# Rewriting a tuned attention and gated-MLP kernel as one scheduled graph: query projections behind the kv sum, paired 64-row remainders, first chunk in halves

## Chip, cores, metric

One core of one Trainium2 chip. The metric is device time in microseconds (us), lower is better. "Span" is the time from the first to the last instruction of one profiled execution; a timed execution is about 1.7 us longer than its own span (238.04 against 236.3). "Granted clock" is the share of TensorE's full clock that the profile recorded. In the lines of the profile PE stands for TensorE's matmuls, PEld for its weight loads, DVE for VectorE, ACT for ScalarE, POOL for GpSimd; a bracket at the end of a line gives the idle time before it and what ended it. PSUM is the memory that matmuls write to; the kernel uses it as eight banks of 512 columns. A run's *state* is fast or slow by its time and clock.

## The reference

A pre-norm block on 2048 tokens of width 448: linear attention with 16 heads of 28 and a softmax feature map, then a gated MLP of width 1792. All inputs are bf16. Abridged:

```python
def _A_ref(x, wqkv, w_phi, wo):
    # q, k, v of x @ wqkv, 16 heads of 28
    pq = jnp.einsum("bhsd,hdf->bhsf", q, w_phi)
    pk = jnp.einsum("bhsd,hdf->bhsf", k, w_phi)
    phi_q = concat([softmax(pq), softmax(-pq)])
    phi_k = concat([softmax(pk), softmax(-pk)])
    kv = jnp.einsum("bhsf,bhsd->bhfd", phi_k, v)   # sum over all tokens: "the kv sum"
    z  = jnp.einsum("bhsf->bhf", phi_k)
    num = jnp.einsum("bhqf,bhfd->bhqd", phi_q, kv)
    den = jnp.einsum("bhqf,bhf->bhq", phi_q, z)[..., None] + 1e-6
    return (num / den).reshape(B, S, D) @ wo

h  = x + _A_ref(layernorm(x), wqkv, w_phi, wo)
h2 = h + (sigmoid(layernorm(h) @ w_gate) * (layernorm(h) @ w_up)) @ w_down
```

Both kernels work in 16 *tiles* of 128 tokens and in *chunks* of four tiles. "num" is the matmul of query features with the kv sum, "item" one block of 128 of the 1792 MLP columns (14 items a chunk) for gate and up together, "down" the last projection, which accumulates 14 matmuls a tile. The width of 448 is three blocks of 128 rows and a remainder of 64: gate and up each need three 128-row matmuls and one 64-row matmul per item. The 64-row matmuls of gate and of up use different halves of the array and can run side by side (in the trace of the kernel before both start at 199.71). The projection matrices of q and k are first multiplied by w_phi in the kernel ("preparation" of the q and k weights).

## The kernel before

The first part is written out by step (a tile per step), with half of the query projections, those of chunks 0 and 1, placed among the steps ahead of the kv sum:

```python
NPQ_A = min(NCH, 2)
for c in range(NPQ_A):
    for g in range(G):
        pq_at.setdefault(4 * c + 3 + O_XT + 1 + 2 * g, []).append((g, c))
pq_deferred = [(g, c) for c in range(NPQ_A, NCH) for g in range(G)]
```

Behind the kv sum, ACT copies num out of PSUM before VectorE works on it:

```python
def a3_copy(t):
    # [cut: waits]
    tk = mark(s_act, act.copy(opm_sb[:, t % NSO, :, :, :].rearrange("p b h e -> p b (h e)"), opm_psum(t)), ("om", t))
```

One gate and up item: two times three full matmuls, then the two 64-row matmuls. ACT takes the sigmoid and copies u, GpSimd multiplies:

```python
def b_gu(f, c):
    # [cut: waits]
    for kt in range(3):
        pe.matmul(banks[bg][:, 0:512], lhsT=wg_sb[:, kt, f * P:(f + 1) * P], rhs=hnT[:, kt, cs], start=(kt == 0), stop=False)
    for kt in range(3):
        pe.matmul(banks[bu][:, 0:512], lhsT=wu_sb[:, kt, f * P:(f + 1) * P], rhs=hnT[:, kt, cs], start=(kt == 0), stop=False)
    pg = pe.matmul(banks[bg][:, 0:512], lhsT=wg_sb[0:64, 3, f * P:(f + 1) * P], rhs=hnT[0:64, 3, cs], start=False, stop=True)
    pu = pe.matmul(banks[bu][:, 0:512], lhsT=wu_sb[64:P, 3, f * P:(f + 1) * P], rhs=hnT[64:P, 4, cs], start=False, stop=True, tile_position=(64, 0))

def b_ucp(f, c):
    tk = mark(s_act, act.copy(u_sb[:, j % 2, :], banks[bu][:, 0:512]), ("ucp", (f, c)))

def b_hh(f, c):
    tk = mark(s_pool, pool.tensor_tensor(hhTc[c][:, f, :], sg_sb[:, j % 2, :], u_sb[:, j % 2, :], ALU.mult), ("hh", (f, c)))
```

The softmax here doesn't subtract the row's maximum and nothing guards it: scores larger than these inputs give would overflow.

## Time and profile before

| | before |
|---|---|
| time, median of 3 runs | 254.34 us (253.8 to 255.51) |
| span of the profiled run, mean granted clock of TensorE | 252.2 us, 0.972 |
| busy: TensorE, VectorE, ACT, GpSimd | 223.5, 127.6, 131.4, 129.9 us |
| exp of tile 0 starts | 15.36 us |
| kv sum masked, ready for num | 63.8 us |
| first gate matmul | 93.44 us |
| last matmul ends, and what follows it | 248.25 us, 4.0 us |

The share of busy time hides that the kernel has three stages with different limits; the last three rows are the borders of these stages.

### The profile page before, as it was taken

What the parts mean: (1) busy time and instruction counts of PE and PEld (TensorE: products, weight loads), DVE (VectorE), ACT (ScalarE), POOL (GpSimd) and SP (SyncE); (2) the same over time, 40 slices, a digit from 0 to 9 for tenths busy, and PEclk for the clock granted to TensorE, in tenths of its full rate; (3) what the DMA queues carried; (4) which work ended last, traced back from release to release, by engine and by line L of the source; (5) the groups of instructions that cost most, each with busy time, mean ns of one, the idle gap of its engine ahead of it and who ended that gap; (6) DMA issues with size and microseconds to landing.
All of it is one profiled execution on the core that took longest, in us unless ns stands there. A gap on an engine that the chain in (4) does not pass through costs nothing.

```text
span 252.2 us, 3761 instructions
## 1 busy us (share of the span) xinstructions
PE 223.5 (89%) x1248; PEld 106.2 (42%) x1248; DVE 127.6 (51%) x344; ACT 131.4 (52%) x258; POOL 129.9 (51%) x145
## 2 busy tenths in 40 slices
PE   1889999994769769979889999899999999999992
PEld 1555656553446334423233454234533345434340
DVE  3566999984497999999999631000100002000003
ACT  2547778871276979945655601763055550154350
POOL 8215687876122445868888601675037660154531
PEclk9999999998668999999999999999999999999999
DMA  6799567530022352332232321000100001100002
GB/s 162 202 326 310 137 171 137 128 83 3 0 42 43 64 106 47 70 73 48 48 67 52 75 62 36 3 0 1 54 19 3 0 3 36 36 1 3 0 0 73
DMA packets 37899, 17.18 MB, mean 68 GB/s; under 512 B 29304, under 2 KB 36984, under 8 KB 37880
## 3 DMA queue, kind: packets, MB, share of 16 engines
q1 hardware_dynamic: 37880, 16.94, 27.6%
q8 instruction: 10, 0.16, 0.3%
q14 instruction: 9, 0.07, 0.1%
HBM read 8.28 MB, written 1.84 MB: 40 GB/s over the span
## 4 chain that ended last, share of the span: by engine, by line
PE 53%; DVE 30%; issue 5%; DMA 5%; ACT 3%; POOL 2%; POOLq 0%; DVEq 0%; ACTq 0%; SPq 0%
PE bank L41 53%; DVE ssum L41 5%; DVE hn_pad L41 5%; DVE mv L41 4%; DVE h_sb L41 3%; DVE rr L41 3%; DVE rden L41 2%; DVE b_sb L41 2%; DMA xnT_50<-xn_pad 2%; DVE xn_pad L41 2%; DVE st L41 2%; POOL phi L41 2%; DMA wqkv_sb<-in_A_wqkv_dram 2%; DVE c_sb L41 1%; DMA x_51<-in_A_x_dram 1%
## 5 line engine op out<-in xcount | busy, mean ns | idle before, releaser
L41 PE MATMUL bank<-hnT,wg_sb 128*128 128x512 bf16 x224 | 65.5, 382 | 4.3 <-ACT u_sb L41 3.5
L41 ACT ACTIVATE sg_sb<-bank 128x512 bf16<-128x512 f32 x56 | 33.4, 596 | 66.8 <-PE bank L41 62.4
L41 PE MATMUL bank<-hnT,wu_sb 128*128 128x512 bf16 x224 | 63.4, 381 | 0.0
L41 DVE TENSOR_TENSOR h_sb<-bank,h_sb 128x448 bf16<-128x448 f32 x16 | 9.7, 623 | 94.6 <-PE bank L41 94.6
L41 PEld LDWEIGHTS bank<-hnT,wg_sb 128*128 128x128 bf16 x224 | 18.6, 96 | 46.9 <-issue 30.7
L41 POOL TENSOR_TENSOR mv<-mv,neghalf 128x1 f32<-128x1 f32 x32 | 18.8, 589 | 33.4 <-DVE mv L41 33.3
L41 ACT CAST u_sb<-bank 128x512 bf16<-128x512 f32 x56 | 32.4, 581 | 0.0
L41 POOL TENSOR_TENSOR hhT_64<-sg_sb,u_sb 128x512 bf16<-128x512 bf16 x14 | 16.2, 1154 | 26.9 <-ACT u_sb L41 26.9
L41 PEld LDWEIGHTS bank<-hnT,wu_sb 128*128 128x128 bf16 x224 | 21.6, 96 | 19.8
L41 POOL TENSOR_TENSOR phi<-ek,ssum 128x896 bf16<-128x896 bf16 x16 | 27.1, 1703 | 1.6 <-DVE ssum L41 1.6
L41 POOL TENSOR_TENSOR hhT_60<-sg_sb,u_sb 128x512 bf16<-128x512 bf16 x14 | 16.1, 1153 | 18.6 <-ACT u_sb L41 18.6
L41 POOL TENSOR_TENSOR o_pad<-c_sb,rden 128x448 bf16<-128x448 bf16 x16 | 15.0, 940 | 18.9 <-DVE rden L41 17.1
L41 POOL TENSOR_TENSOR hhT_56<-sg_sb,u_sb 128x512 bf16<-128x512 bf16 x14 | 16.1, 1159 | 15.4 <-ACT u_sb L41 15.1
L41 ACT CAST opm_sb<-bank 128x960 bf16<-128x960 f32 x16 | 15.6, 975 | 14.1 <-PE bank L41 13.9
L41 DVE TENSOR_SCALAR hn_pad<-h_sb,mv 128x448 bf16<-128x448 bf16 (+1 forms) x32 | 19.7, 659 | 1.3 <-POOL mv L41 1.3
L41 DVE TENSOR_REDUCE ssum<-ek 128x32 f32<-128x896 bf16 x16 | 17.1, 1070 | 2.7 <-ACT ek L41 2.7
L41 POOL TENSOR_TENSOR hhT_52<-sg_sb,u_sb 128x512 bf16<-128x512 bf16 x14 | 17.0, 1217 | 1.6 <-ACT u_sb L41 1.6
L41 PE MATMUL bank<-wo_sb,oT 112*128 112x448 bf16 x64 | 15.6, 367 | 1.9 <-DMA oT<-o_pad 1.0
L41 ACT ACTIVATE junk<-h_sb 128x448 bf16<-128x448 bf16 x16 | 9.4, 588 | 14.4 <-DVE h_sb L41 14.4
L41 ACT ACTIVATE ek<-bank 128x448 bf16<-128x448 f32 x32 | 16.0, 568 | 0.0
L41 DVE TENSOR_TENSOR b_sb<-opm_sb,rr 128x464 bf16<-128x464 bf16 x16 | 13.8, 864 | 0.6
L41 PE MATMUL bank<-wd_sb,hhT_64 128*128 128x448 bf16 x56 | 12.8, 355 | 0.8 <-POOL hhT_64 L41 0.8
(101 smaller groups left out, 309.3 us busy)
## 6 DMA issues: line engine op xcount, KB each, us to landing
out_dram<-h_sb SPq DMA_DIRECT2D x16, 112.0 KB, 1.7
wd_sb<-in_B_w_down_dram SPq DMA_DIRECT2D x7, 224.0 KB, 3.3
wg_sb<-in_B_w_gate_dram SPq DMA_DIRECT2D x3, 448.0 KB, 5.9
wu_sb<-in_B_w_up_dram SPq DMA_DIRECT2D x3, 448.0 KB, 3.9
wqkv_sb<-in_A_wqkv_dram SPq DMA_DIRECT2D x3, 392.0 KB, 3.7
x_51<-in_A_x_dram SPq DMA_DIRECT2D x2, 224.0 KB, 3.0
x_55<-in_A_x_dram SPq DMA_DIRECT2D x1, 448.0 KB
x_59<-in_A_x_dram SPq DMA_DIRECT2D x1, 448.0 KB
```

Source lines behind the costliest of these rows:

```text
L41: ins = getattr(eng, op)(*args, **kw)
```

## The change

The intent: build the whole kernel as one graph of operations with durations and priorities, order it with a list scheduler, and use the freedom for six things. (1) An early start: one tile of x first, filler matmuls. (2) The normalization of the first layer norm moves from VectorE to ACT, its small vectors are done for up to four tiles at once. (3) All 16 query projections go behind the kv sum. (4) VectorE reads num from PSUM and also takes the product of gate and up, so that two kinds of ACT copies and GpSimd's product go. (5) Two items form a pair whose four 64-row matmuls can stand next to each other. (6) The first chunk is cut in halves, so two finished tiles are enough for the first gate matmul. The diff has 1705 lines; its core:

```diff
@@ query projections: 8 of 16 ahead of the kv sum -> all behind it, by priority @@
-            pq_deferred = [(g, c) for c in range(NPQ_A, NCH) for g in range(G)]
+        NPRE = 4
+        pql = [(c, gg) for c in range(NCH) for gg in range(G)]
+        for i, (c, gg) in enumerate(pql[:NPRE]):
+            pq(c, gg, 4 + i % 2, 10 - i * 0.1)
[... cut ...]
+        for i, (c, gg) in enumerate(pql[NPRE:]):
+            pq(c, gg, (4, 5)[i % 2], 12 - i * 0.1)
@@ small vectors of the first layer norm by groups @@
+        groups = [[0], [1], [2, 3]] + [list(range(4 * c, 4 * c + 4)) for c in range(1, NCH)]
@@ chunks @@
+        chunks = [(0, 2), (2, 2)] + [(4 * c, 4) for c in range(1, NCH)]
@@ one item; j is its place in the pair @@
+            def pair(e, st):
+                e.matmul(bk(bg)[:, 0:N], lhsT=wg_sb[0:64, 3, fs], rhs=hb[0:64, 3, ns], start=st, stop=not st)
+                return e.matmul(bk(bu)[:, 0:N], lhsT=wu_sb[64:P, 3, fs], rhs=hb[64:P, 3, ns], start=st, stop=not st,
+                                tile_position=(64, 0))
+            if j == 0:
+                def fn(e):
+                    full(e, wg_sb, bg, True, False)
+                    full(e, wu_sb, bu, True, False)
+                    return pair(e, False)
[... cut: the op "gu" ...]
+            else:
+                def fn1(e):
+                    pair(e, True)
+                    return full(e, wg_sb, bg, False, True)
+
+                def fn2(e):
+                    return full(e, wu_sb, bu, False, True)
[... cut: the ops "gg" and "uu" ...]
@@ product: GpSimd from two SBUF tiles -> VectorE from PSUM @@
-                tk = mark(s_act, act.copy(u_sb[:, j % 2, :], banks[bu][:, 0:512]), ("ucp", (f, c)))
[... cut ...]
-                tk = mark(s_pool, pool.tensor_tensor(hhTc[c][:, f, :], sg_sb[:, j % 2, :], u_sb[:, j % 2, :], ALU.mult),
[... cut ...]
+            op("dve", "hh%d_%d" % (ci, ff), lambda e: e.tensor_tensor(
+                hhT[(t0 // 4) % NHH][:, ff, ns], bk(bu)[:, 0:N], sg_sb[:, k, 0:N], ALU.mult),
@@ down: three chunks in one bank @@
+                if last:
+                    down(t, (3, 2, 6, 7)[i], [2] * 7, 10 - i)
+                else:
+                    down(t, 3, [4, 4, 3, 3], 10)
```

The first item of a pair (op "gu") ends with its 64-row matmuls, the second ("gg", then "uu") begins with them.

## The prediction

> **What bounds the kernel now.** I first cut the span into stretches in the view of engine busy time by window, at the places where the chain of waits changes its engine (us from the start, length, busy time of PE, PEld, DVE, ACT, POOL, granted clock, DMA share, GB/s):
>
> ```profile
> 25.00:55.00 30.00, 29.43 (x219) 18.02 (x217) 27.78 (x65) 23.67 (x52) 23.13 (x20) 1.00 0.60 138
> 55.00:64.00 9.00, 4.44 (x44) 3.16 (x42) 5.15 (x14) 2.65 (x6) 6.10 (x4) 0.82 0.01 2
> 64.00:93.40 29.40, 22.41 (x152) 13.60 (x150) 23.28 (x79) 21.64 (x38) 8.83 (x11) 0.82 0.25 50
> 93.40:130.00 36.60, 34.15 (x183) 13.45 (x184) 35.00 (x100) 23.20 (x47) 26.74 (x29) 1.00 0.30 61
> 160.00:248.30 88.30, 87.26 (x424) 35.51 (x424) 5.58 (x10) 35.94 (x68) 40.32 (x35) 1.00 0.03 11
> ```
>
> There are three regimes. Up to 64 us the first layer norm, the k and v projections and the kv sum. From 64 to 93.4 the attention output without any gate or up matmul to fill TensorE: the first one is at 93.44 in the timeline. From 93.4 to 248.3 the rest, with TensorE nearly always fed. So the end is set by two things: when the first gate matmul can start, and how densely TensorE works from there.
>
> Then the chain of waits in order of time (start, length, what), one period of the first regime:
>
> ```profile
> 26.86 0.50 DVE st L41
> 27.38 0.19 DVE mv L41
> 27.67 0.16 DVE mv L41
> 27.86 0.40 DVE xn_pad L41
> 28.25 1.01 DVE ssum L41
> 29.29 0.35 DVE ssum L41
> 29.64 0.50 DVE st L41
> ```
>
> Statistics, three small vectors, the normalization (0.40), the softmax sums (1.01) and their reciprocal (0.35): 2.78 us a tile, all on VectorE. The "PE busy 29.43" beside it is overlapped matmuls, not a full array.
>
> Last the timeline of TensorE late in the kernel (start, length, engine, operation), one gate and up item:
>
> ```profile
> 198.31 0.82 PE L41 MATMUL bank<-hnT,wg_sb 128*128 128x512 bf16 x3
> 198.97 0.81 PE L41 MATMUL bank<-hnT,wu_sb 128*128 128x512 bf16 x3
> 199.71 0.39 PE L41 MATMUL bank<-hnT,wg_sb 64*128 64x512 bf16 x1
> 199.71 0.39 PE L41 MATMUL bank<-hnT,wu_sb 64*128 64x512 bf16 x1
> 200.03 0.82 PE L41 MATMUL bank<-hnT,wg_sb 128*128 128x512 bf16 x3
> ```
>
> Item to item 1.72. The six full matmuls pace at 0.218 (0.66 for three). The two 64-row matmuls start together, so they are already concurrent. But they start 0.74 after the up triple instead of 0.655, and the next item starts 0.32 later instead of 0.218: 0.19 us an item goes into entering and leaving the 64-row mode.
>
> **What the skill says.** (1) TensorEngine Tiling (Array Packing), Key Properties: "Changing tiling mode (not just tile) drains the TensorE". The 0.19 above agrees. (2) TensorE: Matmul & The Clock Gate, Part 1: an array with too little to do is gated to half rate and comes back after a few busy microseconds. The trace agrees: 448-column matmuls pace 0.37 until about 23 us and 0.19 later, and the granted clock is 0.82 over the two stretches from 55 to 93.4. (3) VectorE: DVE Perf Modes, Why PSUM operands drop a tier: fp32 from PSUM runs at the slowest rate. The trace has 623 ns for the 128x448 final add from PSUM, so a 512-wide product from PSUM should take some 0.69 (estimate, scaled by width with a fixed part of about 0.15). (4) SBUF — State Buffer, Who interferes with whom: VectorE in a two-port mode and GpSimd lock each other out. The trace agrees:
>
> ```profile
> L41 DVE TENSOR_SCALAR hn_pad<-h_sb,mv 128x64 bf16<-128x64 bf16 x16 | 9.2, 578 | 0.0
> L41 POOL TENSOR_TENSOR hhT_52<-sg_sb,u_sb 128x512 bf16<-128x512 bf16 x14 | 17.0, 1217 | 1.6 <-ACT u_sb L41 1.6
> ```
>
> A 64-wide instruction cannot need 578 ns by itself; it waits behind a GpSimd product of 1217.
>
> **The change, part by part.**
>
> *Start.* One tile of x is loaded first instead of two, the small phi weights go out on another queue, filler matmuls warm the array during the loads, and the q weights' preparation (eight copies on ACT, three of them ahead of the first exp today) moves to later. Now exp of tile 0 is at 15.36. After: x lands about 3.3; statistics, rsqrt and bias 1.9; normalization on ACT 0.65 (a 448-wide ACT op is 588 ns); transpose 3.3 (6.78 to 10.10 today); k projection 0.9: about 10.2. Gain 5.
>
> *First regime.* VectorE loses the normalization (0.40 and a gap) and three quarters of the small vectors (grouped by four tiles, about 0.35): 2.78 - 0.42 - 0.35 = 2.0 us a tile. ACT gains 0.5: two exps 0.98, v copy 0.5, normalization 0.5 = 2.0. TensorE needs 8 x 0.19 + 8 x 0.057 = 2.0, GpSimd 1.7 for phi. With four engines at 2.0 in a fixed order, plus the q weights' copies, I take 2.4. Tile 15's exp starts at 10.2 + 15 x 2.4 = 46.2; exp, sums, reciprocal, phi, kv, latencies 1.0 + 1.1 + 0.4 + 1.75 + 0.7 + 0.2 give 51.4; masking kv in two operations instead of eight (1.57 for eight today) 1.2: the kv sum is ready at about 52 instead of 63.8. Gain 12.
>
> *To the first gate matmul.* The chunk of tiles 0 to 3 is cut in halves, so tiles 0 and 1 suffice. For tile 0: num 0.4, VectorE 2.5 (reads PSUM, no ACT copy of 0.97), o 1.1, transpose 2.7, output projection 1.0, residual 0.7, square 0.9, rsqrt 0.8, normalization 0.8, transpose 2.7 = 13.6; tile 1 2.4 behind: 52 + 16 = 68. Today 93.4. Meanwhile the 12 to 16 query projections run, paced by their two exps of about 0.5 each: 12 to 16 us from when ACT is free, about 46. That ends at 58 to 62, hidden, and it keeps the array busy over the gap that halves its clock today.
>
> *TensorE from 68 on.* A pair of items puts its four 64-row matmuls side by side, one mode change in and out instead of two: 12 x 0.218 + 2 x 0.218 + 0.19 = 3.25 instead of 3.44. 21 full pairs: 68.3. The halved chunk: 14 pairs of 1.53 + 0.19 = 24.1. Sum 92.4 against 56 x 1.72 = 96.4: gain 4. Down 224 x 0.19 = 42.5, output projections 13 x 0.76 = 9.9, num 12 x 0.45 = 5.4. Sum 150.2 with no gap. Today's like sum after 93.4 is 96.4 + 42.5 + 7.6 + 1.8 = 148.3 in 154.9: 96% dense.
>
> *What it costs.* The product moves from GpSimd to VectorE and the u copy on ACT goes (56 x 0.58 off ACT, not on the path). VectorE gets 42 x 0.69 + 28 x 0.40 = 40 us, on top of attention at about 4.0 a tile (1.85 small and normalization, 0.6 each for b and c from PSUM, 0.7 residual, gaps) and 10 for the final adds. From 68: 12 x 4.0 + 40 + 10 = 98 of 151. It fits, but until about 130 it is some 85% loaded, and gate and up have only two bank pairs. The first item of a pair gets its banks back after 0.2 + 0.6 (sigmoid) + 0.1 + 0.69 + 0.1 = 1.7, while the other item fills only 1.53. In the crowded part a product also queues behind an attention operation. And down uses one bank for three chunks, so each may wait 0.9 for the final add: at the two switches of the product buffer up to 5 us in all. I take 93% dense: 150.2 / 0.93 = 161.5; 68 + 161.5 = 229.5; the tail after the last matmul is 3.9 today: 233.4. The timed runs are 2.1 above the traced span (254.34 against 252.2), so 235.5; with today's density it would be 230. I say 234.
>
> **Rivals.** *(a) VectorE takes over as the bound*: products are served before attention, so later chunks' inputs come late and TensorE starves. Against: per attention tile TensorE has 1.2 us and VectorE 4.0, and items cost 1.62 against 0.69, which balances at 6.0 us a tile with both full; down adds TensorE work with little VectorE work. For: a fixed order leaves no slack when both are full, and today's VectorE stalls when GpSimd holds the shared port. TensorE at 85%: 245 to 250. *(b) First regime gains nothing*: TensorE, ACT and the transposes (1.2 us each on the sync queue, plus 25 loads of 0.5) become the bound at 2.7; kv ready at 57; about 239. *(c) Everything fits*: first regime at 2.1 and 96% dense: 47 + 16 + 156 + 4 + 2 = 225. *(d) The early start is hidden anyway*: would need TensorE idle later for another reason; the 160 to 248 stretch shows 87.3 of 88.3, so I give it little.
>
> **Range and chances.** Between (c) and a mild (a): 224 to 246. Faster by over 2% means below 249.3; only a strong (a), or a static order that misfits the chip badly, misses that: 0.93. Within 2%: 0.05; slower: 0.02.
>
> **What would show it.** Right: kv masked at 50 to 54, first gate matmul at 65 to 71, no halved clock around it, 64-row matmuls in fours, VectorE above 80% until about 130, TensorE waits of about 0.1 us on products. Wrong: sums still 2.7 apart, a first gate matmul past 80, or TensorE waiting tens of microseconds in total for VectorE.

## The result and the profile after

The changed kernel took **237.62 us** (median of 4 runs, 236.25 to 238.22), the kernel before in the same rounds 254.93 (4 runs). The ratio is **0.930**, with a 95% interval of 0.924 to 0.935. The ratios here are from the fast runs of the same rounds, so not quite those of the medians quoted (237.62 / 254.93 is 0.932). All outputs are right.

| us | before | predicted | after |
|---|---|---|---|
| exp of tile 0 starts | 15.36 | 10.2 | 13.32 |
| exp of tile 15 starts | 56.19 | 46.2 | 52.00 |
| kv sum masked | 63.8 | 52 | 58.17 |
| first gate matmul | 93.44 | 68 | 77.25 |
| last matmul ends | 248.25 | 229.5 | 233.2 |
| span | 252.2 | 233.4 | 236.3 |
| first gate to last matmul | 154.8 | 161.5 | 156.0 |

So the whole gain lies ahead of the first gate matmul (16.2 us). From there to the last matmul the kernel is 1.2 us longer than before: more of num and of the output projections run there now (15.3 us against 9.4 by the sums of the prediction), and the pairs save less than that. The kernel after by stretches (start and end, length, busy time of PE, PEld, DVE, ACT, POOL with counts, granted clock, DMA share, GB/s):

```profile
13.30:52.00 38.70, 33.49 (x259) 20.17 (x259) 31.09 (x60) 30.58 (x63) 26.46 (x17) 0.96 0.78 186
57.00:77.20 20.20, 17.64 (x124) 10.76 (x122) 17.47 (x60) 16.73 (x36) 6.81 (x9) 1.00 0.24 49
93.00:130.00 37.00, 36.52 (x274) 20.97 (x276) 29.84 (x93) 13.94 (x34) 7.63 (x11) 1.00 0.21 43
160.00:233.30 73.30, 70.75 (x347) 29.00 (x350) 23.48 (x37) 13.79 (x24) 0.00 (x0) 1.00 0.06 20
```

In the first line no engine is full: four engines between 68% and 87%, in a fixed order. In the second, where in the kernel before TensorE was busy 76% of the time at a clock of 0.82 (22.41 of 29.40), TensorE, VectorE and ACT are all at 83% to 87%: the query projections have filled it. In the third TensorE is 99% busy and VectorE 81%. Then the kernel after by groups with shapes kept apart (line, engine, operation, operands, count | busy us, mean ns | idle before, releasers):

```profile
L660 DVE TENSOR_TENSOR hhT<-psum,sg_sb 128x512 bf16<-128x512 f32 x42 | 28.7, 690 | 43.7 <-ACT sg_sb L657 27.8 <-PE psum L632 8.3 <-PE psum L670 7.6
L573 DVE TENSOR_TENSOR c_sb<-b_sb,psum 128x464 bf16<-128x464 bf16 x16 | 10.1, 633 | 0.2
L608 DVE TENSOR_SCALAR hn_pad<-x_sb,nm,rst 128x64 bf16<-128x64 bf16 x16 | 4.7, 296 | 0.0
```

The product from PSUM takes 690 ns, as estimated, c from PSUM 633 (0.6 predicted). The small normalization that took 578 ns behind GpSimd's products takes 296. Last, the timeline of TensorE in the kernel after, one pair of items (start, length):

```profile
192.66 0.82 PE L632 MATMUL psum<-xnT,wg_sb 128*128 128x512 bf16 x3
...
195.36 0.39 PE L637 MATMUL psum<-xnT,wg_sb 64*128 64x512 bf16 x1
195.36 0.39 PE L638 MATMUL psum<-xnT,wu_sb 64*128 64x512 bf16 x1
195.59 0.38 PE L637 MATMUL psum<-xnT,wg_sb 64*128 64x512 bf16 x1
195.59 0.38 PE L638 MATMUL psum<-xnT,wu_sb 64*128 64x512 bf16 x1
195.90 0.82 PE L632 MATMUL psum<-xnT,wg_sb 128*128 128x512 bf16 x3
```

195.90 - 192.66 = 3.24 us for two items, against 2 x 1.72 before; that is the 3.25 of the prediction. But counting such clusters over the whole trace, only 21 of the 35 pairs stand side by side; the other 14 times the scheduler put num, an output projection or a down block between the two items. That makes 49 groups of 64-row matmuls against 56 in the kernel before: 7 mode changes saved, 1.3 us at 0.19 each, where the gain of 4 predicted needs 21.

### The profile page after: what moved, and what is told of

It is laid out like the page before. It is cut to its first block, busy times and chain, and to the rows that moved or that the text cites. A ratio compares the mean times of both kernels' runs of the same rounds, so it can differ in the third digit from the quotient of the medians.

```text
span 236.3 us, 3654 instructions
## 1 busy us (share of the span) xinstructions
PE 218.5 (92%) x1371; PEld 111.1 (47%) x1383; DVE 141.0 (60%) x364; ACT 102.3 (43%) x208; POOL 60.2 (25%) x78
## 4 chain that ended last, share of the span: by engine, by line
PE 72%; DVE 10%; DMA 6%; POOL 4%; ACT 4%; issue 2%; SPq 1%; DVEq 0%; POOLq 0%
PE psum L632 33%; PE psum L670 17%; PE psum L637 7%; PE psum L590 5%; POOL phi L469 4%; PE psum L451 3%; PE psum L558 3%; PE psum L485 3%; DMA x_sb<-in_A_x_dram 2%; DMA xnT<-xn_pad 2%; DVE ss L465 2%; DVE hhT L660 1%; DMA xnT<-hn_pad 1%; DVE st L416 1%; PE psum L477 1%
## 5 line engine op out<-in xcount | busy, mean ns | idle before, releaser
L657 ACT ACTIVATE sg_sb<-psum 128x512 bf16<-128x512 f32 (+1 forms) x70 | 35.8, 511 | 83.0 <-PE psum L638 56.7
L660 DVE TENSOR_TENSOR hhT<-psum,sg_sb 128x512 bf16<-128x512 f32 (+1 forms) x70 | 40.4, 584 | 49.5 <-ACT sg_sb L657 31.9
L632 PE MATMUL psum<-xnT,wg_sb 128*128 128x512 bf16 (+1 forms) x202 | 46.8, 338 | 3.1 <-issue 2.4
L632 PE MATMUL psum<-xnT,wu_sb 128*128 128x512 bf16 (+1 forms) x207 | 47.9, 340 | 0.3
L670 PE MATMUL psum<-wd_sb,hhT 128*128 128x448 bf16 x224 | 46.6, 353 | 0.7 <-DVE x_sb L676 0.7
L670 PEld LDWEIGHTS psum<-wd_sb,hhT 128*128 128x128 bf16 x224 | 20.4, 98 | 21.5 <-DVE x_sb L676 2.8
L469 POOL TENSOR_TENSOR phi<-ek,rs 128x896 bf16<-128x896 bf16 x16 | 27.0, 1698 | 10.9 <-DVE rs L467 10.8
L632 PEld LDWEIGHTS psum<-xnT,wu_sb 128*128 128x128 bf16 x210 | 20.7, 99 | 16.0
L637 PE MATMUL psum<-xnT,wg_sb 64*128 64x512 bf16 (+1 forms) x70 | 20.7, 344 | 1.0 <-DVE hhT L660 0.9
L638 PE MATMUL psum<-xnT,wu_sb 64*128 64x512 bf16 (+1 forms) x70 | 20.7, 344 | 0.0
```

The costliest lines, as they stand in the source:

```text
L469: op("pool", "phi%d" % t, lambda e: e.tensor_tensor(phi[:, s, :, :].rearrange("p a (h d) -> p (a h) d", d=DH), ek[:, s, :, :].rearrange("p ...
L632: p = e.matmul(bk(b)[:, 0:N], lhsT=w[:, kt, fs], rhs=hb[:, kt, ns], start=(st and kt == 0), stop=(sp and kt == 2))
L637: e.matmul(bk(bg)[:, 0:N], lhsT=wg_sb[0:64, 3, fs], rhs=hb[0:64, 3, ns], start=st, stop=not st)
L638: return e.matmul(bk(bu)[:, 0:N], lhsT=wu_sb[64:P, 3, fs], rhs=hb[64:P, 3, ns], start=st, stop=not st, tile_position=(64, 0))
L657: op("act", "sig%d_%d" % (ci, ff), lambda e: e.activation(sg_sb[:, k, 0:N], bk(bg)[:, 0:N], ACT.Sigmoid), r=[B(bg)] + (["sigtab"] if sgn[0 ...
L660: op("dve", "hh%d_%d" % (ci, ff), lambda e: e.tensor_tensor(hhT[(t0 // 4) % NHH][:, ff, ns], bk(bu)[:, 0:N], sg_sb[:, k, 0:N], ALU.mult), ...
```

## The experiments

Twelve kernels ran, each timed in five rounds beside the kernel before, on three chips (the kernel before had medians of 253.8 to 255.2 there). The control ran in the first of four sets only, so a difference of medians between sets also holds the difference between chips; the ratios hold less of it, and both are given where they disagree. All but the control are small edits of the kernel after. A table first; "kv" is the start of masking the kv sum, "behind gate" is span minus first gate matmul, both from the profiled run, whose clock stands beside them.

| run | median us | ratio to before [95%] | kv | first gate | behind gate | clock |
|---|---|---|---|---|---|---|
| again (control) | 237.79 | 0.9359 [0.9311, 0.9406] | 57.17 | 77.44 | 159.1 | 0.984 |
| nopair | 243.1 | 0.9573 [0.9523, 0.9623] | 56.53 | 76.80 | 164.0 | 0.986 |
| groups2 | 238.08 | 0.9368 [0.9321, 0.9415] | 57.51 | 77.78 | 159.1 | 0.993 |
| nohalf | 241.68 | 0.9527 [0.9481, 0.9574] | 56.56 | 80.38 | 159.4 | 0.986 |
| adjacent | 235.4 | 0.9257 [0.9220, 0.9293] | 57.33 | 77.61 | 156.1 | 0.985 |
| earlyq | 242.41 | 0.9535 [0.9488, 0.9582] | 60.83 | 78.37 | 161.9 | 0.986 |
| poolprod (one of six runs was slow; median of the five fast) | 244.0 | 0.9567 [0.9510, 0.9624] | 57.37 | 77.65 | 164.6 | 0.986 |
| startfix | 235.57 | 0.9258 [0.9213, 0.9303] | 55.00 | 75.28 | 157.5 | 1.000 |
| onewait | 238.26 | 0.9365 [0.9315, 0.9415] | 57.78 | 78.09 | 158.9 | 0.986 |
| pqbank | 238.05 | 0.9377 [0.9327, 0.9427] | 55.93 | 75.22 | 160.1 | 1.000 |
| combo | 233.19 | 0.9181 [0.9130, 0.9233] | 57.00 | 76.34 | 156.6 | 0.993 |
| combo2 | 231.0 | 0.9042 [0.8993, 0.9091] | 55.93 | 75.28 | 153.4 | 1.000 |

**A warning on the clock, from the control itself.** Its runs differ in how many stretches of half clock they caught: the run with a mean clock of 1.0 has a span of 234.4, the three with 0.986 have 235.8 to 236.1, the one with 0.97 has 237.0. The clock records put one stretch at 3.41 us and 0.986 is two of them, so one costs about 0.8 us by these few runs; in startfix it is 1.1 to 2.0 (234.4 and 234.6 with one stretch, 232.6 to 233.3 with none). Differences of about 1 us between medians can come from that alone; the landmarks of single profiled runs move by about as much. Eight profiled runs have the same order up to the kv sum. Where a stretch fell before it, masking begins at 56.53 to 57.78 (after, again, nopair, adjacent, poolprod, onewait), where none did, at 55.93 and 56.56 (pqbank, nohalf). So the clock is part of that scatter and not all of it.

### again: the kernel after, unchanged

> The changed kernel unaltered, as the yardstick for this set on this chip: ratio 0.930 (0.924 to 0.935 on the chip of the result), span near 236, kv masked near 58, first gate matmul near 77.

It repeated: 237.79 us, kv and first gate within 0.2 us of the first profile.

### nopair: no common mode change

The second item's 64-row matmuls go between its gate and its up triple. Same operations, same order of items, but no two 64-row pairs can meet.

```diff
-                    pair(e, True)
-                    return full(e, wg_sb, bg, False, True)
+                    full(e, wg_sb, bg, True, False)
+                    e.matmul(bk(bg)[:, 0:N], lhsT=wg_sb[0:64, 3, fs], rhs=hb[0:64, 3, ns], start=False, stop=True)
+                    return e.matmul(bk(bu)[:, 0:N], lhsT=wu_sb[64:P, 3, fs], rhs=hb[64:P, 3, ns], start=True, stop=False,
+                                    tile_position=(64, 0))
```

> The order of operations is the same, but the second item of a pair takes its two 64-row matmuls between its gate and its up triple instead of first, so none of the 70 stands beside another item's. In the trace of the changed kernel only 21 of the 35 pairs stand side by side (49 groups of 64-row matmuls, against 56 items before). Theory (the pairing is worth 0.19 us where it happens): 21 x 0.19 = 4.0 us longer, ratio up by 0.016. Rival (TensorE would wait for the products anyway, so the mode changes are hidden): under 1 us, ratio up by less than 0.004.

It took 5.3 us more than the control, all behind the first gate matmul (164.0 against 159.1). The mechanism holds and TensorE is the bound there. Per pair undone that is 5.3 / 21 = 0.25 us, more than the 0.19 that the timeline before gave.

### adjacent: every pair side by side

The scheduler places the second item of a pair at once behind the first, and starts the first only when both can run.

```diff
+        def est2(i):
+            e = est(i)
+            return max(e, est(partner[i]) - ops[i].dur) if i in partner else e
[... cut ...]
+            place(i, e)
+            if i in partner:
+                place(partner[i], max(est(partner[i]), free["pe"]))
```

> The order is changed so that the second item of each gate and up pair always follows the first at once; in the kernel after, only 21 of the 35 pairs do, so 14 mode changes of 0.19 us are bought a second time there. Theory (mode changes cost about 0.19 us each and TensorE is the bound after the first gate matmul): 14 x 0.19 = 2.7 us faster than the unchanged control at 237.8, so about 235.1, ratio to the kernel before about 0.925; the undoing run, which cost 5.3 for 21 pairs, would make it 3.5. The trace should have 35 clusters of 64-row matmuls instead of 49. Rival (the two items were apart because their banks come free one after the other): a pair that must wait for four banks at once waits for the VectorE products instead, and the time is 237 to 240, with idle TensorE time ahead of the first item of a pair up by 3 us or more.

All 35 pairs now form one cluster each, and the time fell by 2.4 us (2.6 by the ratios): 0.17 to 0.19 per mode change saved. The intervals of the two ratios do not overlap. The rival, a wait for four banks at once, did not show: TensorE's idle time behind the first gate matmul is 3.0 us, in the control 3.3. In the control the timeline of TensorE looks like this; the remainder at 97.10 stands alone, the two at 98.73 and 98.85 are a pair, the one at 103.12 is alone again:

```profile
97.10 0.28 PE L637 MATMUL psum<-xnT,wg_sb 64*128 64x256 bf16 x1
...
98.73 0.28 PE L637 MATMUL psum<-xnT,wg_sb 64*128 64x256 bf16 x1
...
98.85 0.27 PE L637 MATMUL psum<-xnT,wg_sb 64*128 64x256 bf16 x1
...
103.12 0.28 PE L637 MATMUL psum<-xnT,wg_sb 64*128 64x256 bf16 x1
```

### nohalf: the first chunk whole

```diff
-        chunks = [(0, 2), (2, 2)] + [(4 * c, 4) for c in range(1, NCH)]
+        chunks = [(4 * c, 4) for c in range(NCH)]
```

> The first chunk is one piece of four tiles again. Theory (the early start matters because TensorE has nothing else to do there): first gate matmul 4 to 6 us later, 1.3 us given back because 7 pairs of half items fewer change mode, 3 to 4 us longer in all, ratio up by 0.012 to 0.016. Rival (TensorE has query projections and attention to fill the gap): within 1 us.

The first gate matmul came 2.9 us later (4 to 6 expected; the chain from masking to it is 23.8 us instead of 20.3) and the time rose by 3.9 us. Behind it two things cancel: TensorE idles 6.5 us instead of 3.3, and has 35 groups of 64-row matmuls instead of 49. The profiled run also has a stretch of 6.83 us at half clock from 79.44 on, the control one of 3.41 at that place. Halving pays, although it doubles the number of that chunk's items.

### groups2: the hole in the first regime

In the kernel after, the exps of tiles 7 and 8 are 7.85 us apart (28.00 and 35.85). The timeline of VectorE at that place:

```profile
29.05 1.65 DVE L429 SCALAR_TENSOR_TENSOR nb<-mv,rst 128x4 f32<-128x4 f32 x1
```

and that of ACT:

```profile
28.44 0.54 ACT L461 ACTIVATE ek<-psum 128x448 bf16<-128x448 f32 x1
30.74 2.06 ACT L435 ACTIVATE xn_pad<-x_sb,nb,rst 128x448 bf16<-128x448 bf16 x3 [1.76 <-DVE nb L429]
```

ACT waits 1.76 us for a four-element vector that takes VectorE 1.65 us instead of the 0.16 of the next one (36.36); it ends together with a GpSimd operation that began just before it (28.99 to 30.69). No run tests that link. The small vectors of four tiles come at once, and late. So I made the groups two tiles:

```diff
-        groups = [[0], [1], [2, 3]] + [list(range(4 * c, 4 * c + 4)) for c in range(1, NCH)]
+        groups = [[0], [1]] + [[t, t + 1] for t in range(2, NT, 2)]
```

> The first layer norm takes its inverse roots for two tiles at a time instead of four. In the changed kernel the exp of tile 7 is at 28.0 and that of tile 8 at 35.9, 7.9 us for one tile, behind the inverse roots and the normalization of tiles 8 to 11. Theory (the hole comes from the grouping and the first regime sets the start of all that follows): the hole shrinks to some 4 us, kv masked 3 to 4 us earlier, first gate matmul likewise, time 3 to 4 us shorter (ratio down by 0.012 to 0.016). Rival (ACT and VectorE at 2.2 to 2.3 us a tile are the limit and catch up): kv masked within 1 us of before and the time unchanged.

The hole was gone (no step between exps above 5 us), but the kv sum came no earlier and the time was the same. My theory fell. VectorE is busy 33.3 us of the 38.7 us from 13.3 to 52 where the control has 30.8, with 64 instructions instead of 59: the hole was probably bought back with more work on small vectors. Its runs even had the better clock (0.991 to 1.0), and its profiled run no half clock before the kv sum, which came 0.9 to 1.6 us later than in pqbank and nohalf. A visible gap in a chain of four nearly full engines need not be worth anything.

### startfix: the loads of x planned with measured latencies

```diff
-               dur=0.5, prio=prio, dma="in", lat=1.8 + (b - a) * 0.45, nring=32,
+               dur=0.5, prio=prio, dma="in", lat=(5.3 if a == 2 else 4.0 if a == 1 else 5.6 if a == 4 else 1.8 + (b - a) * 0.45), nring=32,
```

> Only the order is changed: the loads of x are planned with the latencies that the trace shows (5.3 us for the second piece), so that the VectorE copies of the k weights no longer stand behind the statistics of tiles 2 and 3. Theory (the late start is passed on to the kv sum): first exp 1.5 to 2 us earlier than in the control (13.3), last kv matmul 1 to 2 us earlier than 56.5, time 236 to 236.8. Rival (as the run with groups of two showed: the sum of work on ACT and VectorE sets the kv sum, and an early start only fills a hole): first exp earlier, last kv matmul within 0.5 us of 56.5, time within 0.8 us of 237.8.

The scheduler had believed that tiles 2 and 3 land after 2.7 us. They took 5.25, and VectorE stood before their statistics while the copies of the k weights waited behind them in program order. The timeline of VectorE in the control:

```profile
8.05 0.63 DVE L416 BATCH_NORM_STATS2 st<-x_sb 128x6 f32<-128x448 bf16 x1 [1.10 <-DMA x_sb<-in_A_x_dram]
8.59 0.67 DVE L383 COPY WkT<-psum 112x448 bf16<-112x448 bf16 x2
```

and in startfix:

```profile
6.16 0.39 DVE L383 COPY WkT<-psum 112x448 bf16<-112x448 bf16 x1 [0.66 <-PE psum L375]
...
7.00 0.38 DVE L383 COPY WkT<-psum 112x448 bf16<-112x448 bf16 x1
```

The first exp came at 11.64 instead of 13.36, the kv sum 2.2 us earlier, the time fell by 2.2. Not all of it is the start: the profiled run was at full clock, and against pqbank and nohalf, which have the control's order up to there and no half clock, the kv sum is 0.9 and 1.6 us earlier. At equal full clock the spans are 232.6 to 233.3 against the control's one 234.4. So 1.1 to 1.8 us come from the order and the rest from fewer stretches of half clock.

### earlyq: half of the query projections ahead of the kv sum again

```diff
-            pr = 90 if w == 0 else 30
+            pr = 90 if w == 0 else 43
-        NPRE = 4
+        NPRE = 8
-            pq(c, gg, 4 + i % 2, 10 - i * 0.1)
+            pq(c, gg, 4 + i % 2, 41 - i * 0.1)
```

> Half of the query projections (the first 8 of 16) and the preparation of their weights get a priority that puts them ahead of the kv sum again. Theory (before the kv sum the first regime is full on ACT and VectorE, and behind it the projections are hidden beside the attention): the last kv matmul comes 6 to 8 us later than in the unchanged control (56.5), the attention behind it is 1 to 3 us shorter, the first gate matmul comes 4 to 6 us later and the time is 242 to 244. Rival 1 (what is moved is moved one for one: the projections share ACT and VectorE with the attention behind the kv sum, so moving them only shifts the wait): kv 6 to 8 later, kv to gate 6 to 8 shorter, 237 to 239. Rival 2 (the first regime has room for them): kv unchanged, gate earlier, below 236.

The total was as the theory said (242.41, 4.6 us slower), the way there was not. By the trace 12 of the 16 projections now run ahead of the masking, in the control 3. The kv sum came only 3.7 us later, the chain behind it got 2.7 us shorter (17.5 from masking to first gate, 20.3 in the control), so the first gate moved by 0.9 us only. The loss came behind it: 161.9 against 159.1, and it is mostly a by-product of the new order: one output projection more lies there (13 instead of 12, 0.76 us each), only 19 pairs stand side by side (21 in the control), TensorE idles 0.5 us more, and a stretch of 6.83 us at half clock begins at 77.29 (in the control one of 3.41 at 78.94). What each costs is not separated. So the 4.6 us are not the price of the place of the projections alone; at the first gate matmul that price is 0.9. The view by stretches shows why it is small. earlyq:

```profile
62.00:78.40 16.40, 9.15 (x76) 5.31 (x74) 14.47 (x51) 7.58 (x15) 5.62 (x8) 0.97 0.22 43
```

The control:

```profile
57.00:77.40 20.40, 17.83 (x127) 10.87 (x124) 17.50 (x60) 16.94 (x37) 6.81 (x9) 1.00 0.25 53
```

With all but four of the projections done, TensorE works 9.2 of 16.4 us; the attention is a chain of latencies through VectorE (the waits of TensorE list 4.2 us for b_sb). With 13 of them it works 17.8 of 20.4. So the projections are neither free nor hidden behind the kv sum. They lengthen that stretch, but it has room for most of them and the stage before it has less.

### poolprod: the product back on GpSimd, u copied by ACT

```diff
-            op("dve", "hh%d_%d" % (ci, ff), lambda e: e.tensor_tensor(
-                hhT[(t0 // 4) % NHH][:, ff, ns], bk(bu)[:, 0:N], sg_sb[:, k, 0:N], ALU.mult),
+            op("act", "uc%d_%d" % (ci, ff), lambda e: e.copy(u_sb[:, k, 0:N], bk(bu)[:, 0:N]), r=[B(bu)], w=[("ub", k)],
+               dur=0.15 + 0.4 * u, prio=50)
+            op("pool", "hh%d_%d" % (ci, ff), lambda e: e.tensor_tensor(
+                hhT[(t0 // 4) % NHH][:, ff, ns], u_sb[:, k, 0:N], sg_sb[:, k, 0:N], ALU.mult),
```

> The product of gate and up goes back to GpSimd, with ACT copying u out of PSUM first, as in the kernel before; the rest stays. Theory (the product on VectorE is paid for by what ACT and GpSimd lose, and a bank is held shorter): GpSimd products of 1.2 us for 512 columns hold the port that VectorE shares, small VectorE operations go from about 300 to about 580 ns and the small operations on GpSimd queue behind the products; the first gate matmul stays within 1 us of 77.4, and the time after it grows by 3 to 8 us: 241 to 246. Rival (VectorE is the crowded engine behind the first gate matmul until about 150, so taking 40 us off it lets the attention of later chunks go faster): 234 to 237.

(The port is that of point 4 of the prediction.) The time rose by 6.2 us (5.3 by the ratios), with the first gate matmul where it was. VectorE's total work fell from 140.8 to 109.9 us and it did not help: the products on GpSimd took 1155 ns, and VectorE's normalizations were slow again, as the groups of poolprod show (in the kernel after 391 and 296 ns):

```profile
L608 DVE TENSOR_SCALAR hn_pad<-x_sb,nm,rst 128x448 bf16<-128x448 bf16 x16 | 9.2, 576 | 2.2 <-POOL rst L604 2.1
...
L609 DVE TENSOR_SCALAR hn_pad<-x_sb,nm,rst 128x64 bf16<-128x64 bf16 x16 | 8.0, 500 | 0.0
```

The order was planned anew with GpSimd's durations, so how much of the 6.2 is VectorE held up by GpSimd and how much the longer way from matmul to product is not separated. Behind the first gate matmul TensorE idles 7.7 us instead of 3.3; the named waits are for the transpose of o (2.3), the final add (2.2) and the copy of u (2.1).

### onewait and pqbank: what holds the first gate matmul

In the control TensorE sits idle 1.88 us before the first gate matmul, and the profile names no releaser. Its timeline there:

```profile
75.19 0.37 PE L558 MATMUL psum<-kvz,eq 112*128 112x120 bf16 x4
77.44 0.49 PE L632 MATMUL psum<-xnT,wg_sb 128*128 128x256 bf16 x3 [1.88 <-issue]
```

Counted in the program, this matmul has eleven waits: two transposed tiles, the last exp of the query projections (whose bank it takes), and eight weight loads, long landed. Either the eight waits cost something, or the exp does. Two edits, one for each:

```diff
+            if i < 8:                                            # onewait
+                g.ops[-1].sem, g.ops[-1].val = ("gu", 0), 16 * (i + 1)
```

```diff
-            pq(c, gg, (4, 5)[i % 2], 12 - i * 0.1)
+            pq(c, gg, (4, 3)[i % 2], 12 - i * 0.1)               # pqbank; the first four alike
```

> The first gate matmul waits on eleven semaphores in a row: two transposes, the last exp of the query projections (whose bank it takes) and eight weight loads that landed long before. In every run so far TensorE sits idle for exactly 1.88 us before it, put down to issue. Here the eight loads count on one semaphore, so eight waits become one; nothing else changes, the order neither. Theory A (each wait instruction costs TensorE's queue some 0.16 us even when it is long fulfilled): idle falls to about 0.7, first gate matmul at about 76.2 instead of 77.4, time 0.5 to 1.2 below 237.8. Theory B (the wait is for the last exp of the query projections, which ends 0.2 us before the first gate matmul): idle stays 1.88, time within 0.4 of 237.8.

> The query projections use PSUM bank 3, free at that time, instead of bank 5, so that the last of them holds no bank that the first gate item takes. Theory B (the first gate matmul waits for the bank of the last query projection): the first gate matmul moves from 77.4 to about 76.2 to 76.5, 0.1 to 0.3 behind the landing of the second transposed tile; the sigmoid still waits for the last exp and its table (78.5), so the time falls by 0.3 to 1.2. Theory A (eleven waits in a row cost the queue): first gate matmul within 0.3 of 77.4, time within 0.4 of 237.8.

Removing seven of the eleven waits changed nothing: idle 1.92, time 238.26. With fewer waits the profile now names the releaser, and it is the exp. With the bank changed the idle time halves, and the profile names the transpose. The timeline of TensorE in onewait:

```profile
78.09 0.49 PE L634 MATMUL psum<-xnT,wg_sb 128*128 128x256 bf16 x3 [1.92 <-ACT eq L492]
```

and in pqbank:

```profile
75.22 0.49 PE L632 MATMUL psum<-xnT,wg_sb 128*128 128x256 bf16 x3 [0.90 <-DMA xnT<-hn_pad]
...
77.12 0.93 PE L590 MATMUL psum<-wo_sb,oT 112*128 112x448 bf16 x4 [0.87 <-DMA oT<-o_pad]
```

The timeline of ACT in pqbank, up to the last but one query projection:

```profile
74.42 0.59 ACT L492 ACTIVATE eq<-psum 112x512 bf16<-112x512 f32 x1
```

So theory B is right on the wait: masking to first gate fell from 20.3 to 19.3 us. The transpose is not the new releaser, though. It landed at 74.75, while the exp above ends at 75.01 and the first gate matmul follows 0.21 us later, exactly as it follows the last exp in the control (77.23, then 77.44). The first gate item takes banks 4 and 5; pqbank moved the last projection off bank 5, but the one before it still uses bank 4. In combo and combo2 the profile names the exp at this place (0.95 us). And the edit bought nothing: 238.05 us. The order now puts an output projection behind the first item, TensorE waits 0.87 us for that, and only 19 pairs stand side by side instead of 21. The gain was given back at once.

### combo and combo2: together

combo has the edits of adjacent, startfix, onewait and pqbank. combo2 adds one line: down alternates between two banks, once the output projections no longer need the second.

```diff
-                    down(t, 3, [4, 4, 3, 3], 10)
+                    down(t, 3 if t < 4 else (3, 2)[t % 2], [4, 4, 3, 3], 10)
```

> What helped, together: pairs always side by side, loads of x planned with measured latencies, one semaphore for the gate and up weights, query projections off the first gate item's bank. If the gains add (2.4 from the pairs, 2.2 from the start, up to 1 from the first gate): 232 to 233.5, ratio about 0.916. If they overlap because TensorE then waits for VectorE products (the attention of later chunks and the products share it until 150): 234.5 to 235.5, no better than the best of the two.

> The combined kernel (233.19, ratio 0.9181) with the down projections of tiles 5 to 11 alternating between PSUM banks 3 and 2; tiles 0 to 3 keep bank 3, since bank 2 takes the output projections until then. In the trace of the combined kernel TensorE idles 2.2 us in 3 places, 0.7 each, where a down projection waits for the final add of the tile before it in the one bank, with 4.7 us in 6 places of waiting ahead of weight loads, partly beside matmuls. Theory (those waits are on the path): 1.5 to 2.5 us faster, 230.7 to 231.7, ratio about 0.910, and the waits of down for the final add are gone. Rival (they are bought back as waits for the last products of a chunk, which down needs too): within 0.6 of 233.2.

The gains of adjacent and startfix add up: 233.19, 4.6 us under the control, as the sum of 2.4 and 2.2 says. At full clock it is less: three runs of combo have spans of 230.9 to 231.0, the control's one 234.4, so 3.5 us. At the first gate matmul the early start and the changed bank do not add up: combo2, at full clock, has it at 75.28, startfix alone at 75.28 and pqbank alone at 75.22. The second bank for down gave 2.2 us more (3.5 by the ratios, whose intervals do not overlap; 2.2 to 3.2 by the spans of the runs at full clock): **231.0 us, ratio 0.904**, the best version here and 2.8% under the kernel after. Of the waits of TensorE behind the first gate matmul, the largest in combo (engine, line waited for, us in total, times, longest):

```profile
PE psum L688 <- DVE x_sb L694: 2.2, 3, 0.7
```

and the two largest in combo2:

```profile
PE psum L608 <- DMA oT<-o_pad: 1.5, 2, 0.8
PE psum L650 <- DVE hhT L678: 0.5, 1, 0.5
```

The 2.2 us of down waiting for the final add of the tile before are gone, and no other wait took their place (the transpose of o had the same 1.5 in combo, the product hhT 0.2); the gain of 2.2 in the medians is of that size.

## Why the prediction was right, and where not

It said 234.0 within 224 to 246, and 237.6 came. The total is right, partly because two errors cancel: the first gate matmul came 9.25 us late, and the part behind it took 5.5 us less than said. That is luck. Most of its own signs of being right failed: the kv sum was ready at 58.2 (50 to 54 said), the first gate matmul was at 77.3 (65 to 71), a stretch of half clock began at 77.65, and VectorE was busy 79% from there to 130 (above 80%). None of its signs of being wrong came either. The offset of 2.1 between timed run and span is 1.7 run by run.

**The start was sized wrong (10.2; it was 13.3).** The step counted x, statistics, normalization, transpose and k projection, and overlooked that the k weights must be ready too and that their copies can stand behind a statistic that waits for its load. startfix shows that the misplanned load accounts for 1.7 of the 3.1 us.

**The first regime was too fast (2.4 us a tile; it was 2.58).** The mechanism, VectorE losing work and four engines coming near to balance, held. So did the sums: from 13.3 to 52 ACT is busy 30.6 us and VectorE 31.1, 2.04 and 2.07 a tile against 2.0 said, although one normalization on ACT takes 0.76 us and not 0.5. What was too small is the allowance for four engines waiting on each other, 0.4 a tile; over 15 tiles the difference is 2.7 us. Which waits make it up stays open: the gap in the middle is not the cause (groups2), and the clock is at most a part (2.50 and 2.55 a tile in pqbank and nohalf, without half clock there).

**That the query projections run hidden and end at 58 to 62 failed.** Their matmuls ran from 53 to 75, and the first gate matmul waited for the exp of the last one (onewait, pqbank). The work was sized rightly: 32 exps of about 0.48 on ACT are 15 us (12 to 16 said). But they were let start at 46 and run undisturbed. The first exp was at 54.0, behind the first regime's, and they were spread over 23.0 us among the attention, with ACT busy 16.7 of the 20.2 us. This step should have added up the stretch per engine: 14 us of projections on TensorE and 15 on ACT, in a stretch predicted to be 16 us long that also holds the attention of the first tiles. It took 19.1 us from the masked kv sum to the first gate instead of 16; with 12 projections done ahead (earlyq) it took 16.4. Together the three steps (3.1, 2.7 and 3.1, and 0.4 in between) make up the 9.25 us by which the first gate came late; the 0.4 is a slip of its sum, where 51.4 and 1.2 give 52.6 and not 52. The direction was right all the same, but by little: undoing it in part (earlyq) costs 0.9 us at the first gate matmul, and the 4.6 in all are mostly lost behind it.

**"93% dense" was too pessimistic, and this cancelled more than half of it.** The work of 150.2 us (152.9 with the 14 mode changes that were not saved) ran in 156.0. Rival (a), VectorE as the new bound, took hold of little: in the control TensorE's listed waits for VectorE behind the first gate are 0.9, 0.7 and 0.7 us (those of its weight loads, partly beside matmuls, 4.9, 3.8 and 2.8). And moving the product to VectorE was a net gain (poolprod), and VectorE's own stalls behind GpSimd went with it; the prediction had named that stall, but counted only the cost of the move.

**The pairs side by side, gain 4, were right per pair and wrong in number.** A pair takes 3.24 us (3.25 said). But only 21 pairs stand side by side, which the graph leaves to the scheduler. The run that forces all 35 gains the missing 2.4 us, the run that forbids all loses 5.3.

**That down may wait for its one bank, up to 5 us in all,** was right in kind. The run with a second bank gained 2.2 us by the medians.

**The halved chunk** is worth 3.9 us (nohalf); the prediction counted it only inside the chain to the first gate.

What stays open: which waits make a tile of the first regime 2.58 us, why nopair costs 0.25 us per pair where adjacent gains 0.17 to 0.19, and how poolprod's 6.2 us divide. No run undoes the early start, the normalization on ACT or the reading of num from PSUM. So of the 16.2 us gained ahead of the first gate matmul, the 5.6 up to the kv sum (63.8 to 58.17) are not divided among the parts, and of the 10.5 behind it (29.6 to 19.1) only the 3.5 of the halved chunk are shown (nohalf). The effects of the parts (5.3, 3.9, 4.6, 6.2 us when undone) sum to more than the whole gain of 17 us, so they are not independent.

## What to carry to other kernels

Before calling work hidden behind a wait, add it up for every engine in that stretch, ask from when that engine is really free, and look at whose bank or queue it sits in; the filler may then be what the next stage waits for. A gap in a timeline or a named wait is a place to experiment, not a gain: of three that looked worth 1 to 4 us, only the one-bank wait of down paid. In a statically ordered program, feed the scheduler with latencies from the trace, and force the adjacency that the gain rests on.

## What the Trainium skill lacked or had wrong

- TensorEngine Tiling (Array Packing), Key Properties, says that a mode change drains TensorE and gives no size there. These runs: 0.19 us for entering and leaving together by the timeline, 0.17 to 0.19 per one saved (adjacent), 0.25 per one added (nopair).
- TensorE: Matmul & The Clock Gate, Part 1, gives the window as 3.41 us and free-running, and the clock records agree: stretches of 3.41 and 6.83 us at half clock, differing between runs of one kernel. The Terms of that page reckon the penalty as the throttled time times the share withheld, about 1.7 us for a stretch of 3.41 (estimate from the page). The control paid less, about 0.8 us each (spans of 234.4, 235.8 to 236.1 and 237.0 at mean clocks of 1.0, 0.986 and 0.97), startfix 1.1 to 2.0.
- On no page that I found: a releaser named "issue" can be a real wait that the profile could not attribute. The same wait of 1.9 us was put down to issue while the matmul had eleven waits, and to the exp when it had four.
